# Softmax block kernel: sums of values in 64x32 tiles, one half of the keys at a time

## The chip, the cores and the metric

The kernel runs on one core of one Trainium2 chip. The metric is the device time of one execution in microseconds (us). The core's TensorE (PE) multiplies, and its weight loads are shown on their own row (PEld). VectorE (DVE), ScalarE (ACT), GpSimd (POOL) and the DMA queues, here issued by SyncE (SP), do the rest.

## The reference

One transformer block with an adaptive layer norm on 2048 rows of 512 values: 32 heads of 16 values, then a layer of 1792 hidden units.

```python
mod = (silu(c) @ w_mod).reshape(1, 6, 1, 512)          # sa, ca, ga, sb, cb, gb
h = layernorm(x) * (1 + ca) + sa
q, k, v = split(h @ wqkv)                              # 32 heads, 16 values each
p = softmax(q @ k.T * 16**-0.5)                        # 2048 x 2048 for each head
x = x + ga * ((p @ v) @ wo)
h = layernorm(x) * (1 + cb) + sb
x = x + gb * (gelu(h @ w1 + b1) @ w2 + b2)
```

All arrays are float32.

## The kernel before

The attention is cut into 32 units: four blocks of 512 queries (`TB`) times eight groups of four heads. Each unit runs through 16 chunks of 128 keys, so that the main loop has 32 x 16 = 512 steps. Before it, the inputs, the first projections and the first maxima are prepared; after it, the last block of rows goes through the output projection and the two layers of the feed-forward part.

A step works at three things in turn for attention.

- `exp_mm` (L589) makes scores with the keys on the partitions: 128 keys x 512 queries for one head. Its operands are 50 rows high (three parts of a split product of 16 rows each, and two rows that subtract the maximum). A head lies on partitions 0 to 63 or 64 to 127, so that a product uses one half of the rows of the array, in a 64x128 tile. ACT then takes the exponential into a tile `p` (L594), from a ring of twelve. Four such products belong to a step.
- `mx_mm` (L393) makes scores of a coming unit with the queries on the partitions, 48 rows high and again in a 64x128 tile. DVE reduces each to a maximum for its 128 queries (L398). Four belong to a step.
- `pv_step` (L618) multiplies the four tiles `p` of the step before with the values: 128 keys high, 32 columns wide for each head (16 values, a column of ones that gives the sum of the exponentials, and padding). The four heads stand in four 128x32 tiles side by side, all 128 rows high, and add into one bank of PSUM over the 16 chunks. These operands are full float32, and every product shows as two records in the profile.

After the sixteenth chunk `attn_out` copies the bank to SBUF by ACT (L606) and sends it to memory.

Beside that runs work of the other matrix products, "bg": the remaining projections, the output projection and the feed-forward part, as groups of split products that add to one bank each. They too are cut into halves of 64 rows (L287, `bg_mm`), because they are meant to stand in one half of the array while scores stand in the other. `half_step` issues six of them (`RUN`) in one step, all on one half, which changes with each step, and puts a score product on the other half behind each. When it has issued what the step owes, it calls `pv_step`.

The order in which the engines take all this is the order of the calls (`manual_schedule`). `later(n, f)` puts an action n exponentials later. `saw` notes the first ACT instruction behind a run of bg products; the run on the other half waits for it, since both halves add to one bank.

The eight banks of PSUM in the loop are dealt out by rings:

```python
ring("e", (0, 1, 2))
ring("mx", (3, 4, 5))
ring("pv", (6,))
ring("bg", (7,))
```

Of the kernel before, what the change touches and what calls it, by code (L numbers as in the profile page):

```python
# [7 lines left out]
F32 = mybir.dt.float32  # L8
FR = mybir.dt.float32r
AF = mybir.ActivationFunctionType  # L10
ALU = mybir.AluOpType
# [4 lines left out]
P = 128  # L16
# [8 lines left out]
TB = S // NB  # L25
HS = S // 2
NKC = S // P
NG = H // 4
NU = NB * NG
VW = DH + 1  # L30
# [10 lines left out]
RUN = 6  # L41
# [8 lines left out]
def block_kernel(ctx: ExitStack, tc: tile.TileContext, x, wqkv, wo, w1, b1, w2, b2, c, w_mod, out):  # L50
    nc = tc.nc
    te, ve, ac, gp, sy = nc.tensor, nc.vector, nc.scalar, nc.gpsimd, nc.sync
    ctx.enter_context(tc.manual_schedule())

    def pool(name, bufs=1, **kw):
        cm = tc.tile_pool(name=name, bufs=bufs, **kw)
        return cm, cm.__enter__()
# [8 lines left out]
    def bank(i, name):  # L66
        return bank_pools[i].tile([P, TB], F32, tag=f"bank{i}", name=name)
# [3 lines left out]
    def ring(name, ids):  # L71
        rings[name], turn[name] = list(ids), 0

    def take(name):
        ids = rings[name]
        turn[name] += 1
        return bank(ids[(turn[name] - 1) % len(ids)], name)
# [6 lines left out]
    ou_d = [dram.tile([NG, P, TB], F32, name=f"ou{b}") for b in range(NB)]  # L84
# [25 lines left out]
    kqcm, kqpool = pool("kq")  # L110
# [166 lines left out]
    def later(n, f):  # L277
        hooks.setdefault(clock["t"] + n, []).append(f)

    def advance():  # L280
        clock["t"] += 1
        for f in hooks.pop(clock["t"], []):
            f()
# [67 lines left out]
    def kh(u, h):  # L351
        return khalf[(2 * u + h) % 5]
# [28 lines left out]
    xc, red, mrows = [0, 0], {}, set()  # L381

    def mx_mm(a):

        u, i = XFIRST[xc[a]] if xc[a] < 64 else divmod(xc[a], 32)
        xc[a] += 1
        kr, p, qc = i // 8, (i // 4) % 2, i % 4
        if u not in mxp:
            mxp[u] = small.tile([P, 16, 4], F32, tag="mxp", name="mxp")
            red[u] = 0  # L390
        ps = take("mx")
        r0 = a * 64
        te.matmul(ps, qst[u][r0 : r0 + KR, p, qc * P : (qc + 1) * P],  # L393
                  kh(u, kr // 2)[r0 : r0 + KR, p, (kr % 2) * TB : (kr % 2 + 1) * TB], start=True, stop=True)
        hc = (a * 2 + p) * 4 + qc

        def reduce():
            ins = ve.tensor_reduce(mxp[u][:, hc, kr : kr + 1], ps, axis=AX.X, op=ALU.max, negate=True)  # L398
            red[u] += 1
            if red[u] == 64:  # L400
                max_rows(u)
            return ins

        return reduce

    def max_rows(u):
        m = mn[u % 2]
        ve.tensor_reduce(m[:, :16], mxp.pop(u), axis=AX.X, op=ALU.min)
        mt = small.tile([P, 32], F32, tag="mt", name="mt")
        ve.transpose(mt, m)  # L410
        m2 = small.tile([P, 2, 32], FR, tag="m2", name="m2")
        gp.tensor_copy(m2[:, 0], mt)  # L412
        gp.tensor_tensor(m2[:, 1], mt, m2[:, 0].bitcast(F32), op=ALU.subtract)

        def store():
            for i in range(2):
                sy.dma_start(m_d[u][i].rearrange("x b j -> b x j"), m2[:, i].bitcast(F32))

        def load():
            mrows.add(u)  # L420
            for a in range(2):
                r0 = a * 64 + KR
                sy.dma_start(qst[u][r0 : r0 + 2].bitcast(F32).rearrange("s p t -> s (p t)"),
                             m_d[u][:, a * 8 : a * 8 + 8].rearrange("s x b j -> s (x b j)"))

        if u:
            later(5, store)
        else:
            store()
        later(11 if u else 2, load)  # L430
# [104 lines left out]
    ppcm, ppool = pool("p", bufs=12)  # L535
    vg, pt = {}, {}
# [31 lines left out]
        preps.append((w2[f * P : (f + 1) * P, :], w2_d[f], gb_b))  # L568


    ring("e", (0, 1, 2))
    ring("mx", (3, 4, 5))
    ring("pv", (6,))
    ring("bg", (7,))
    ec, begun = [0, 0], [0]
    cur = {"pv": 0}

    def exp_mm(a, bk="e"):

        s, p = divmod(ec[a], 2)  # L580
        while begun[0] < min(ec) // 2 + 1:
            begun[0] += 1
            step_start(begun[0] - 1)
        ec[a] += 1
        u, kc = divmod(s, NKC)
        assert u in mrows, (u, ec, xc, red, clock["t"])
        r0 = a * 64
        ps = take(bk)
        te.matmul(ps, kh(u, kc // 8)[r0 : r0 + KX, p, (kc % 8) * P : (kc % 8 + 1) * P], qst[u][r0 : r0 + KX, p],  # L589
                  start=True, stop=True)  # L590

        def act():
            t = ppool.tile([P, TB], F32, tag="p", name="p")
            saw(ac.activation(t, ps, AF.Exp, scale=SCALE))  # L594
            pt[4 * s + p * 2 + a] = t
            advance()

        return act

    done = [-1] * NB  # L600
    ready = []

    def attn_out(u, pv):
        qb, g = divmod(u, NG)
        o = kqpool.tile([P, TB], F32, tag="osb", name="osb", bufs=1)
        saw(ac.activation(o, pv, AF.Copy))  # L606
        later(2, lambda: sy.dma_start(ou_d[qb][g], o))
        if g % 2:
            later(8, lambda: ready.append((qb, g // 2)))

    def pv_step():
        s = cur["pv"]
        cur["pv"] += 1
        u, kc = divmod(s, NKC)
        if kc == 0:
            cur["ps"] = take("pv")
        for j in range(4):
            te.matmul(cur["ps"][32 * j : 32 * (j + 1)], vg[u][:, kc, j * VW : j * VW + 32], pt.pop(4 * s + j),  # L618
                      start=kc == 0, stop=kc == NKC - 1)
        if kc == NKC - 1:  # L620
            vg.pop(u)
            attn_out(u, cur["ps"])


    pools = {}
# [68 lines left out]
    stream, at = [], 0  # L694
    for b in range(NB):
        stream += [(b, "o", k) for k in range(KC)]
        at = 0
        for lo, hi in PARTS:
            top = min(hi + AHEAD, NF)
            stream += [(b, 1, i) for i in range(at, top)] + [(b, 2, i) for i in range(lo, hi)]  # L700
            at = top
# [172 lines left out]
    act = {"g": None}  # L874

    def saw(ins):

        if act["g"] and not act["g"]["seen"]:
            act["g"]["seen"] = ins.ins

    def bg_mm(h):

        g = act["g"]
        terms, bk, evac = g["group"]
        i = g["at"][h]
        if i == len(terms):
            return False
        if g["n"] == 0:
            g["ps"] = take(bk)
        ins = mm(g["ps"], terms[i], g["n"], 2 * len(terms), slice(h * 64, h * 64 + 64)).ins  # L890
        if g["n"] and g["half"] != h:
            tc.add_manual_dep(ins, g["seen"].name, AFTER, reason="both halves of the rows add to one bank")
        g["half"], g["seen"] = h, None
        g["at"][h] += 1
        g["n"] += 1
        if g["n"] == 2 * len(terms):
            evac(g["ps"])
            act["g"] = None
        return act["g"] is not None

    def half_step(hs):
        h = hs % 2
        if h:
            wload()
        if act["g"] is None:
            j = next(jobs, None)
            if callable(j):
                j()
            elif j is not None:
                act["g"] = {"group": j, "at": [0, 0], "n": 0, "seen": None}  # L910
        nx = min(64 * NU, LEAD + 4 * (hs + 1))
        ne = 4 * (hs + 1)

        def x_ok(a):
            return sum(xc) < nx and xc[a] < 32 * NU

        def e_ok(a):
            return sum(ec) < ne and ec[a] < 2 * NU * NKC

        more = act["g"] is not None  # L920
        free = not more
        k = 0
        while more and k < RUN:
            a = 1 - h
            more = bg_mm(h)
            if e_ok(a) and sum(ec) < ne - 1 and (k % 2 == 1 or not x_ok(a)):
                exp_mm(a)()
            elif x_ok(a):
                mx_mm(a)()
            k += 1  # L930
        while sum(ec) < ne or sum(xc) < nx:
            a = 0 if ec[0] <= ec[1] else 1
            fs = []
            if sum(ec) < ne:
                fs.append(exp_mm(a, "bg" if free and sum(ec) == ne - 1 else "e"))
                if x_ok(1 - a):
                    fs.append(mx_mm(1 - a))
                elif e_ok(1 - a):
                    fs.append(exp_mm(1 - a))
            else:  # L940
                fs += [mx_mm(i) for i in range(2) if x_ok(i)]
            for f in fs:
                f()
        if hs:
            assert min(ec) >= 2 * cur["pv"] + 2
            pv_step()

    pend = []

# [12 lines left out]
        try_prep()  # L962

    for hs in range(NU * NKC):
        half_step(hs)
    if act["g"]:
        while bg_mm(1 - hs % 2):
            pass
    pv_step()
    while act["g"]:  # L970
        bg_mm(hs % 2)
    close(ppcm, vgcm)


    ring("bg", (0, 1, 2, 3, 4, 5, 7))
    tcm, tpool = pool("tail")
    extra += [tpool.tile([P, 2, D], FR, name=f"wt{i}") for i in range(6)]
    x2_t += [tpool.tile([P, D], F32, name=f"x2t{i}") for i in range(4)]
# [14 lines left out]
    left, j = True, None  # L993
    while left or j != "ffn":
        if j != "ffn":
            j = next(last)
# [3 lines left out]
        i = next(jobs, 0)  # L1000
# [32 lines left out]
```

## Time and profile before

| | |
|---|---|
| median of 3 runs | 1830.92 us (1827.09 to 1833.09) |
| profiled execution | 1831.95 us, span 1829.8 us |
| mean granted TensorE clock | 0.973 |
| PE busy | 1752.0 us, 96% |
| DVE busy | 1403.7 us, 77% |
| ACT busy | 1210.8 us, 66% |
| POOL busy | 602.5 us, 33% |

The profile is of one execution. The span runs from the first to the last instruction. In a timeline each row has a start and a length in us, the engine, the line of the kernel, the operation, what it writes and reads, the shape, and how many instructions are drawn together. Matmuls are pipelined: a record of 0.39 us does not keep its tile for that long, and the pace is read from the starts. The ends of matmuls are modelled.

### The profile page before, as it was taken

The page shows a single profiled execution, that of the slowest core. Times are in us where ns is not written, and L with a number is a line of the kernel's source. Part 1 is how long each engine was busy: PE and PEld are TensorE (multiplying, and loading weights), DVE is VectorE, ACT ScalarE, POOL GpSimd, SP SyncE. Part 2 cuts the span into 40 slices and gives each one's busy share as a digit, 9 for nine tenths or more (in the row PEclk, how much of TensorE's full clock was granted, in tenths as well). Part 3 has the DMA queues.
Part 4 walks back from the last instruction along what each step waited for, and adds up shares of the span by engine and source line. Part 5 has one row for each costly group of instructions (what it writes and reads, how often), then busy time and mean ns, then how long its engine had stood idle before and what let it go on. Part 6 is the DMA issues. An engine that isn't in the chain of part 4 may idle for free. (4 is left out here: it accounts for less than half of the span.)

```text
span 1829.8 us, 32358 instructions
## 1 busy us (share of the span) xinstructions
PE 1752.0 (96%) x12032; PEld 905.0 (49%) x12032; DVE 1403.7 (77%) x2347; ACT 1210.8 (66%) x2303; POOL 602.5 (33%) x640
## 2 busy tenths in 40 slices
PE   7798999999999899999999899999999899999899
PEld 5475444444434344444444344444444444445677
DVE  4466888888898788888899888888889888850232
ACT  2324777777676678778777688778776678777031
POOL 2413544543100246206410246306420136405420
PEclk9798999999899899999999899999999999999999
DMA  6647777777633434346446444336446434312544
GB/s 196 202 122 203 217 184 203 209 192 188 181 80 69 89 89 110 75 94 158 108 102 183 103 108 107 83 87 155 106 96 192 111 64 109 97 35 97 182 156 161
DMA packets 122906, 242.62 MB, mean 133 GB/s; under 512 B 30982, under 2 KB 50454, under 8 KB 122750
## 3 DMA queue, kind: packets, MB, share of 16 engines
q1 hardware_dynamic: 122750, 240.57, 50.3%
q8 instruction: 95, 1.56, 0.4%
q14 instruction: 61, 0.50, 0.1%
HBM read 187.61 MB, written 52.90 MB: 131 GB/s over the span
## 5 line engine op out<-in xcount | busy, mean ns | idle before, releaser
L398 DVE TENSOR_REDUCE mxp<-mx 128x1 f32<-128x512 f32 x2048 | 1272.7, 683 | 203.7 <-PE mx L393 184.0
L594 ACT ACTIVATE p<-e 128x512 f32<-128x512 f32 x1967 | 1029.4, 603 | 358.8 <-PE e L589 305.4
L393 PE MATMUL mx<-kh,qst 48*128 48x512 f32 x2048 | 873.8, 444 | 26.4 <-DVE mxp L398 19.9
L589 PE MATMUL e<-qst,kh 50*128 50x512 f32 x1967 | 716.9, 419 | 5.1 <-issue 4.8
L618 PE MATMUL pv<-p,vg 128*32 128x512 f32 x4096 | 553.9, 613 | 0.0
L589 PEld LDWEIGHTS e<-qst,kh 50*128 50x128 f32 x1967 | 359.7, 188 | 173.3 <-ACT p L594 150.8
L393 PEld LDWEIGHTS mx<-kh,qst 48*128 48x128 f32 x2048 | 376.7, 187 | 76.6 <-DVE mxp L398 71.0
L287 PE MATMUL bg<-w,g 64*128 64x512 f32 (+1 forms) x1020 | 274.3, 406 | 3.4 <-DVE x L830 1.0
L287 PE MATMUL bg<-pc,w 64*128 64x512 f32 (+1 forms) x984 | 270.3, 407 | 1.4 <-DVE x L830 0.7
L287 PEld LDWEIGHTS bg<-w,g 64*128 64x128 f32 (+1 forms) x1020 | 179.3, 186 | 146.3 <-ACT p L594 82.2
L287 PEld LDWEIGHTS bg<-pc,w 64*128 64x128 f32 (+1 forms) x984 | 169.5, 184 | 160.9 <-ACT p L594 98.8
L618 PEld LDWEIGHTS pv<-p,vg 128*32 128x32 f32 x4096 | 81.1, 108 | 129.6 <-issue 122.8
L412 POOL CAST m<-mt 128x32 fp32r<-128x32 f32 x32 | 6.7, 209 | 369.6 <-DVE mt L410 369.6
L287 PE MATMUL bg<-hThi,wqk 64*128 64x512 f32 x352 | 107.2, 424 | 0.3 <-ACT p L594 0.3
L804 POOL TENSOR_SCALAR s<-s 128x512 f32<-128x512 f32 x42 | 63.0, 1500 | 132.2 <-ACT s L802 124.0
L287 PEld LDWEIGHTS bg<-hThi,wqk 64*128 64x128 f32 x352 | 59.6, 188 | 80.5 <-ACT p L594 73.7
L797 POOL TENSOR_TENSOR s<-h 128x512 f32<-128x512 f32 x42 | 43.7, 1041 | 120.1 <-ACT h L796 119.9
L287 PE MATMUL bg<-wo,pc 64*128 64x512 f32 x288 | 81.9, 412 | 1.0
L287 PEld LDWEIGHTS bg<-wo,pc 64*128 64x128 f32 x288 | 49.5, 184 | 48.3 <-ACT p L594 27.7
L670 POOL TENSOR_TENSOR ob<-ob,rb 128x512 f32<-128x512 f32 x12 | 15.4, 1283 | 171.1 <-DMA rb<-rden 111.3
L773 ACT ACTIVATE h<-bg,modc 128x512 f32<-128x512 f32 x16 | 12.1, 778 | 67.5 <-PE bg L771 41.7
L807 POOL TENSOR_TENSOR g<-h,g 128x512 fp32r<-128x512 f32 x42 | 53.9, 1284 | 3.4
(128 smaller groups left out, 1267.3 us busy)
## 6 DMA issues: line engine op xcount, KB each, us to landing
kh<-qk SPq DMA_DIRECT2D x366, 128.0 KB
w<-w1s SPq DMA_DIRECT2D x56, 512.0 KB
w<-w2s SPq DMA_DIRECT2D x51, 512.0 KB
vg<-v SPq DMA_DIRECT2D x32, 664.0 KB
qk<-parts SPq DMA_DIRECT2D x32, 512.0 KB
qst<-qk SPq DMA_DIRECT2D x192, 64.0 KB
ou<-osb SPq DMA_DIRECT2D x32, 256.0 KB
wo<-wos SPq DMA_DIRECT2D x15, 512.0 KB
```

The lines of the kernel that those rows point to most:

```text
L287: return te.matmul(ps, term[0][r], term[1][r], start=i == 0, stop=i == n - 1)
L393: te.matmul(ps, qst[u][r0 : r0 + KR, p, qc * P : (qc + 1) * P], kh(u, kr // 2)[r0 : r0 + KR, p, (kr % 2) * TB : (kr % 2 + 1) * TB], start= ...
L398: ins = ve.tensor_reduce(mxp[u][:, hc, kr : kr + 1], ps, axis=AX.X, op=ALU.max, negate=True)
L412: gp.tensor_copy(m2[:, 0], mt)
L589: te.matmul(ps, kh(u, kc // 8)[r0 : r0 + KX, p, (kc % 8) * P : (kc % 8 + 1) * P], qst[u][r0 : r0 + KX, p], start=True, stop=True)
L594: saw(ac.activation(t, ps, AF.Exp, scale=SCALE))
L618: te.matmul(cur["ps"][32 * j : 32 * (j + 1)], vg[u][:, kc, j * VW : j * VW + 32], pt.pop(4 * s + j), start=kc == 0, stop=kc == NKC - 1)
L670: eng.tensor_tensor(ob, ob, rb, op=ALU.mult)
L773: ac.activation(h, ps, AF.Identity, scale=modc[:, 1, fc, 0:1], bias=modc[:, 1, fc, 1:2])
L797: gp.tensor_tensor(s, h, h, op=ALU.mult)
L804: gp.tensor_scalar(s, s, 1.0, None, op0=ALU.add)
L807: gp.tensor_tensor(g[:, 1], h, g[:, 0].bitcast(F32), op=ALU.subtract)
```

## The change

The sums of values are no longer taken over all 128 keys of a chunk at once. `pv_half(h)` takes the four heads over the 64 keys on partitions 0 to 63 or 64 to 127, in 64x32 tiles; the two halves add into two banks of their own, bank 6 and bank 2. Bank 2 is taken from the ring of scores for the exponentials, which is left with two. `attn_out` copies both banks by ACT and adds them on POOL, and what follows it is put off by four exponentials more.

`half_step` becomes `step`, with an order that is written out. With bg products, and h for their half and o for the other: bg beside a maximum, bg beside an exponential's score, both once more, then the sum of values on o, two bg and a score on h, the sum of values on h, and three scores on o. Without bg products: the sum on h, four scores on o, the sum on o, four scores on h. The sums lag two steps behind the scores instead of one. The half on which the six bg products stand still changes with each step.

```diff
-    ring("e", (0, 1, 2))
+    ring("e", (0, 1))
     ring("mx", (3, 4, 5))
-    ring("pv", (6,))
+    ring("pv", (6, 2))
     ring("bg", (7,))
...
     def attn_out(u, pv):
         qb, g = divmod(u, NG)
-        o = kqpool.tile([P, TB], F32, tag="osb", name="osb", bufs=1)
-        saw(ac.activation(o, pv, AF.Copy))
-        later(2, lambda: sy.dma_start(ou_d[qb][g], o))
+        o = [pl.tile([P, TB], F32, tag=f"osb{h}", name=f"osb{h}", bufs=1) for h, pl in enumerate((kqpool, ppool))]
+        for h in range(2):
+            saw(ac.activation(o[h], pv[h], AF.Copy))
+        gp.tensor_tensor(o[0], o[0], o[1], op=ALU.add)
+        later(6, lambda: sy.dma_start(ou_d[qb][g], o[0]))
...
-    def pv_step():
-        s = cur["pv"]
-        cur["pv"] += 1
+    def pv_half(h):
+        s = pvc[h]
+        pvc[h] += 1
         u, kc = divmod(s, NKC)
-        if kc == 0:
-            cur["ps"] = take("pv")
+        assert min(ec) >= 2 * s + 2
+        if u not in sums:
+            sums[u] = [take("pv"), take("pv")]
+        r = slice(h * 64, h * 64 + 64)
         for j in range(4):
-            te.matmul(cur["ps"][32 * j : 32 * (j + 1)], vg[u][:, kc, j * VW : j * VW + 32], pt.pop(4 * s + j),
+            te.matmul(sums[u][h][32 * j : 32 * (j + 1)], vg[u][r, kc, j * VW : j * VW + 32], pt[4 * s + j][r],
                       start=kc == 0, stop=kc == NKC - 1)
...
+        h = act["g"]["n"] // RUN % 2 if more else 0
...
+        def pv(a):
+            if hs > 1:
+                pv_half(a)
...
+        o = 1 - h
+        if more:
+            order = ((bg,), (x, o), (bg,), (e, o), (bg,), (x, o), (bg,), (e, o), (pv, o), (bg,), (bg,), (e, h),
+                     (pv, h), (x, o), (e, o), (x, o))
+        else:
+            order = ((pv, h), (x, o), (e, o), (x, o), (e, o), (pv, o), (x, h), (e, h), (x, h), (e, h))
+        for f, *a in order:
+            f(*a)
```

`x` issues a product for a maximum, `e` one for an exponential, `bg` one of the six products of other work.

More of the change, by code (lines that the diff above doesn't have):

```diff
@@ L568, in block_kernel @@
         preps.append((w2[f * P : (f + 1) * P, :], w2_d[f], gb_b))
-    ring("e", (0, 1, 2))
+    ring("e", (0, 1))
     ring("mx", (3, 4, 5))
-    ring("pv", (6,))
+    ring("pv", (6, 2))
     ring("bg", (7,))
     ec, begun = [0, 0], [0]
-    cur = {"pv": 0}
+    pvc, sums = [0, 0], {}
     def exp_mm(a, bk="e"):
@@ L604, in attn_out @@
         qb, g = divmod(u, NG)
-        o = kqpool.tile([P, TB], F32, tag="osb", name="osb", bufs=1)
-        saw(ac.activation(o, pv, AF.Copy))
-        later(2, lambda: sy.dma_start(ou_d[qb][g], o))
+        o = [pl.tile([P, TB], F32, tag=f"osb{h}", name=f"osb{h}", bufs=1) for h, pl in enumerate((kqpool, ppool))]
[3 more added lines that the diff above has]
+        later(6, lambda: sy.dma_start(ou_d[qb][g], o[0]))
         if g % 2:
-            later(8, lambda: ready.append((qb, g // 2)))
-    def pv_step():
-        s = cur["pv"]
-        cur["pv"] += 1
+            later(12, lambda: ready.append((qb, g // 2)))
+    def pv_half(h):
+        s = pvc[h]
+        pvc[h] += 1
         u, kc = divmod(s, NKC)
-        if kc == 0:
-            cur["ps"] = take("pv")
+        assert min(ec) >= 2 * s + 2
+        if u not in sums:
+            sums[u] = [take("pv"), take("pv")]
+        r = slice(h * 64, h * 64 + 64)
         for j in range(4):
-            te.matmul(cur["ps"][32 * j : 32 * (j + 1)], vg[u][:, kc, j * VW : j * VW + 32], pt.pop(4 * s + j),
+            te.matmul(sums[u][h][32 * j : 32 * (j + 1)], vg[u][r, kc, j * VW : j * VW + 32], pt[4 * s + j][r],
                       start=kc == 0, stop=kc == NKC - 1)
-        if kc == NKC - 1:
-            vg.pop(u)
-            attn_out(u, cur["ps"])
+        if min(pvc) > s:
+            for j in range(4):
+                pt.pop(4 * s + j)
+            if kc == NKC - 1:
+                vg.pop(u)
+                attn_out(u, sums.pop(u))
     pools = {}
@@ L899, in bg_mm, with step @@
         return act["g"] is not None
-    def half_step(hs):
-        h = hs % 2
-        if h:
+    def step(hs):
+        if hs % 2:
             wload()
@@ L910, in half_step, with x, e, bg @@
                 act["g"] = {"group": j, "at": [0, 0], "n": 0, "seen": None}
+        more = act["g"] is not None
+        h = act["g"]["n"] // RUN % 2 if more else 0
         nx = min(64 * NU, LEAD + 4 * (hs + 1))
         ne = 4 * (hs + 1)
[L914 to L928, printed above, removed]
+        def x(a):
+            if sum(xc) < nx and xc[a] < 32 * NU:
                 mx_mm(a)()
[L930 to L933, printed above, removed]
+        def e(a):
             if sum(ec) < ne:
[L935 to L946, printed above, removed]
+                a = a if ec[a] < 2 * NU * NKC else 1 - a
+                exp_mm(a, "bg" if not more and sum(ec) == ne - 1 else "e")()
+        def pv(a):
+            if hs > 1:
+                pv_half(a)
+        def bg():
+            bg_mm(h)
+        o = 1 - h
[6 more added lines that the diff above has]
+            f(*a)
+        while sum(xc) < nx:
+            x(0 if xc[0] <= xc[1] else 1)
+        assert sum(ec) == ne
     pend = []
@@ L964, in block_kernel @@
     for hs in range(NU * NKC):
[L965 to L969, printed above, removed]
+        step(hs)
+    for h in range(2):
+        pv_half(h)
+    h = act["g"]["n"] // RUN % 2 if act["g"] else 0
+    while act["g"] and act["g"]["at"][h] < len(act["g"]["group"][0]):
+        bg_mm(h)
+    for i in range(2):
+        pv_half(i)
     while act["g"]:
-        bg_mm(hs % 2)
+        bg_mm(1 - h)
     close(ppcm, vgcm)
-    ring("bg", (0, 1, 2, 3, 4, 5, 7))
+    ring("bg", (0, 1, 3, 4, 5, 7, 2))
     tcm, tpool = pool("tail")
```

## The prediction

> **What bounds the kernel now.** I read the page's first part, then its groups, then who waited for whom on TensorE, then a steady stretch of the timeline.
>
> ```profile
> span 1829.8 us, 32358 instructions
> PE 1752.0 (96%) x12032; PEld 905.0 (49%) x12032; DVE 1403.7 (77%) x2347; ACT 1210.8 (66%) x2303; POOL 602.5 (33%) x640
> ...
> L398 DVE TENSOR_REDUCE mxp<-mx 128x1 f32<-128x512 f32 x2048 | 1272.7, 683 | 203.7 <-PE mx L393 184.0
> L594 ACT ACTIVATE p<-e 128x512 f32<-128x512 f32 x1967 | 1029.4, 603 | 358.8 <-PE e L589 305.4
> ```
> ```profile
> PE mx L393 <- DVE mxp L398: 19.9, 13, 4.6
> ```
>
> TensorE is busy for 96% of the span, its longest wait in total is 19.9 us, and DVE idles for 203.7 us in front of the maxima, mostly for TensorE. The bound is TensorE's stream. A busy share does not say how well it is packed, so I read two steps by starts.
>
> ```profile
> 901.91 1.07 PE L618 MATMUL pv<-p,vg 128*32 128x512 f32 x8
> 902.90 0.50 PE L287 MATMUL bg<-w,g 64*128 64x512 f32 x1
> 902.91 0.49 PE L393 MATMUL mx<-kh,qst 48*128 48x512 f32 x1
> 903.24 0.40 PE L589 MATMUL e<-qst,kh 50*128 50x512 f32 x1
> 903.24 0.62 PE L287 MATMUL bg<-w,g 64*128 64x512 f32 x2
> 903.48 0.40 PE L393 MATMUL mx<-kh,qst 48*128 48x512 f32 x1
> 903.71 0.39 PE L287 MATMUL bg<-w,g 64*128 64x512 f32 x1
> ...
> 904.17 0.39 PE L287 MATMUL bg<-w,g 64*128 64x512 f32 x1
> 904.18 0.69 PE L589 MATMUL e<-qst,kh 50*128 50x512 f32 x2
> 904.41 0.48 PE L393 MATMUL mx<-kh,qst 48*128 48x512 f32 x1
> 904.82 1.06 PE L618 MATMUL pv<-p,vg 128*32 128x512 f32 x8
> 905.82 0.50 PE L287 MATMUL bg<-w,g 64*128 64x512 f32 x1
> ```
> ```profile
> 902.90 0.18 PEld L287 LDWEIGHTS bg<-w,g 64*128 64x128 f32 x1 [0.84 <-ACT p L594]
> 902.90 0.18 PEld L393 LDWEIGHTS mx<-kh,qst 48*128 48x128 f32 x1
> 903.01 0.19 PEld L287 LDWEIGHTS bg<-w,g 64*128 64x128 f32 x1
> ```
> ```profile
> L618 PE MATMUL pv<-p,vg x4096: 592/616/1062, 162.8 to 1688.8; 128*32 128x512 f32 x196
> ```
>
> From one block of sums to the next is 904.82 - 901.91 = 2.91 us: the step. Seven pairs of 64x128 products stand in it, each pair one product on either half of the rows. Inside, pairs start every (904.41 - 903.24) / 5 = 0.234 us, so 7 x 0.234 = 1.64 us. The block of sums costs the rest, **1.27 us**. Its eight records (two for each of four products; 4096 in 512 steps) come in two waves: the block lasts 1.07 us and a record 0.592 to 0.617 us, so the second four start about 0.46 us after the first, and two waves are 0.92 us. The remaining 0.35 us lies at the borders. The last pair before the sums is followed only after 0.41 us instead of 0.23; the first pair behind them comes 0.99 us after their start, and the second pair 0.34 us after that instead of 0.23. The weight row tells why: the weight rows idle for 0.84 us during the sums, and the first weights of the next shape load at 902.90, when the sums are through. Between pairs of one shape weights load ahead (903.01 for 903.24). So at a change of the tile's shape TensorE runs empty before even weights of the new shape move.
>
> How many steps are of this kind:
>
> ```profile
> L287 PE MATMUL bg<-pc,w 64*128 64x512 f32 x960 | 264.5, 408 | 1.4 <-DVE x L830 0.7 <-ACT p L594 0.6
> L287 PE MATMUL bg<-w,g 64*128 64x512 f32 x816 | 226.0, 409 | 3.4 <-DVE x L830 1.0
> L287 PE MATMUL bg<-hThi,wqk 64*128 64x512 f32 x352 | 107.2, 424 | 0.3 <-ACT p L594 0.3
> L287 PE MATMUL bg<-wo,pc 64*128 64x512 f32 x288 | 81.9, 412 | 1.0
> ...
> L287 PE MATMUL bg<-hTlo,wqk 64*128 64x512 f32 x176 | 47.7, 390 | 0.0
> ```
>
> The half products of other work number 960 + 816 + 352 + 288 + 176 = 2592, six to a step: **432 steps with them, 80 without**. A step without them:
>
> ```profile
> 1449.24 2.48 DVE L398 TENSOR_REDUCE mxp<-mx 128x1 f32<-128x512 f32 x4 [0.18 <-PE mx L393]
> ...
> 1450.42 1.07 PE L618 MATMUL pv<-p,vg 128*32 128x512 f32 x8
> ...
> 1453.15 1.06 PE L618 MATMUL pv<-p,vg 128*32 128x512 f32 x8
> ```
>
> It takes 1453.15 - 1450.42 = 2.73 us, near the 2.48 us of its four maxima on DVE. 432 x 2.91 + 80 x 2.73 = 1475 us, against 1526 us from the first sums to the last (162.8 to 1688.8). The other 51 us are stalls between.
>
> **The change part by part.**
>
> *The sums cut in halves.* Four products 128 rows high become eight, 64 high, and each still streams 512 columns in two waves. So there are two blocks of 0.92 us, each filling half the array, where one block filled all of it. That costs nothing if the other half works meanwhile, and 0.92 us a step if it does not. The order written out offers that: three 64x128 products stand behind each block on the other half. All hangs on whether a 64x32 product on one half and a 64x128 product on the other are in the array together.
>
> The trace of before has no 64x32 product. The nearest rows are the borders above: between 128x32 and 64x128 even the weights wait until the array is empty. There both shapes share rows, here they don't. But a conflict of rows alone would not hold back weights, which between equal shapes on the same rows load ahead; it looks like a barrier on the shape. The Trainium skill, TensorEngine Tiling (Array Packing), section Tiling Modes, Key Properties, says that changing the tiling mode, not just the tile, drains the engine, and it lists 64x128 and 64x32 as two configurations; the trace agrees for 128x32 against 64x128 (0.35 us of borders a step), and by this rule the sum is the 2770 us below, without it the 1700 us of the first rival.
>
> I take the barrier. Then a step has four borders instead of two, and nothing stands beside the sums. A step with other work becomes: three scores on o together with the next step's first four bg and four scores. The next step's bg stands on the old o, so the longer chain there is 3 + 4 = 7 products, 7 x 0.234. Then a block; then two bg and a score, all on one half, 3 x 0.234; then a block. That is 10 x 0.234 + 2 x 1.27 = 4.88 us, **1.97 us more**, of which 0.70 is the three products that lost their partners and 1.27 the second block. 432 x 1.97 = 851 us. A step without other work: 8 x 0.234 + 2 x 1.27 = 4.41 us, 1.68 more, 80 times: 134 us.
>
> The block's price has two ends: 1.27 us, as above; and 0.99 us, from its start to the next product's, if nothing else of the borders is added. The low end gives 4.32 and 3.85 us, so 432 x 1.41 + 80 x 1.12 = 699 us instead of 985. I take 1.27, since it is the row's full price with the same neighbours, 64x128 on both sides.
>
> *The stalls.* In steps of 4.9 us DVE (2.48 us) and ACT are far from late, and loads have longer to land, so I take the 51 us off; the other end is to leave them.
>
> *Two banks for scores instead of three, twelve tiles p with a lag of two steps.* A bank is held for a product (0.39 us) and an exponential (0.60): 0.99 / 2 = 0.50 us a score, four in 1.98 us. Steps of 2.91 or 4.88 us hide that; at 2.5 us it would show whenever ACT does something else. The twelve tiles now hold exactly the three steps between a score and the end of its sums, so the first exponential of a step waits for the block on h of the step before; ACT's copies for other work queue behind it. In the order of issue that block stands ahead of the exponential's own product anyway, so with a barrier the wait is over when the product ends. Zero here.
>
> *The copy of the sums.*
>
> ```profile
> L606 ACT ACTIVATE osb<-pv 128x512 f32<-128x512 f32 x32 | 19.3, 603 | 5.0 <-PE pv L618 3.1
> L670 POOL TENSOR_TENSOR ob<-ob,rb 128x512 f32<-128x512 f32 x12 | 15.4, 1283 | 171.1 <-DMA rb<-rden 111.3
> ```
>
> 32 more copies of 0.60 us on ACT and 32 additions of about 1.28 us on POOL. ACT is busy 66% and POOL 33%, so both hide, but POOL is in order: the addition waits for both copies, and the products and subtractions of the hidden layer queue behind it. They have actions of ten exponentials (over 7 us) between them, which cover it. The store of the sums waits four exponentials more on SP's queue. Only the last unit has no cover: 0.6 + 1.28, about 2 us at the start of the tail. The rest of the tail uses other shapes and is as before.
>
> The sum: 1831.95 (the profiled execution, 1 us above the median of 1830.92) + 851 + 134 + 2 - 51 = **2768, say 2770 us**. Its own range: 1832 + 699 + 2 - 51 = 2480 with the low block, and 1832 + 987 = 2819 with all stalls kept, to which I add 30 for what the steps may lose elsewhere: 2480 to 2850.
>
> **The rivals.**
>
> *No barrier between 64x32 and 64x128; faster.* Both halves run through 7 products and one block with no borders: 7 x 0.234 + 0.92 = 2.56 us, just over DVE's 2.48. 432 x 0.35 = 151 us less: 1683. At that pace DVE, the two banks and TensorE take turns in being late by up to some 0.15 us a step (half the slack gone), 65 us, so 1683 to 1748, and I put it at 1700. For it: 48- and 50-row products already stand beside 64-row ones in one pace, so the halves are independent in one shape. Against: the weights held back at every border seen. It decides from the point where a block's borders cost under 0.35 us in each half while the other half goes on.
>
> *Together in the array, but no gain; slower by a little.* Each half pays its own borders (0.35 us a step, as now), so the step stays at 2.91, and the two banks show behind each ACT copy of another product: at most 0.60 us for each of 432 / 4 groups, 65 us, so 1834 to 1899. If moreover products start in the order of issue, whatever half they are on, then the three behind a block wait until its second wave has started, and a step is 10 x 0.234 + 0.92 = 3.26 us: 151 us more, 1985. I put this at 1900. The Trainium skill, TensorE: Matmul & The Clock Gate, Part 3, The mechanism, holds that matmuls start and end strictly in program order, which would make the 1985 the likelier end here; no row here shows one half waiting in that way.
>
> **How the numbers follow.** The barrier 0.50, together without gain 0.19, no barrier 0.31. One case of each sign has much of the chance, and nothing lies between but the second rival. The range leaves out what may lie above 2850 and the lower half of the faster case: 1695 to 2850; the likeliest case's own range is 2480 to 2850. A run can tell 0.3%, 5.5 us, from no change. Faster 0.31 is the first rival. A small part of the second ends within 0.3%: 0.03. Slower: 0.66.
>
> **What would show it.** Right: in the timeline of the changed kernel no 64x128 product starts while a block of sums streams; blocks are 0.9 to 1.3 us long, two to a step, with weight loads idle over each; steps of about 4.9 us; DVE falls to about half busy; the first two bg behind a block stand alone. For the first rival: 64x32 records and 64x128 records start within one another, steps of 2.5 to 2.7 us, DVE over 90% busy. For the second: they overlap, but the step stays near 2.9 or 3.3 us, with waits of scores on ACT. I am wrong altogether if the block on 64 rows is not as long as that on 128, or if products of other work fall behind and run in the tail.

## The result, and the profile after

The changed kernel takes 4634.92 us (median of 4 runs, 4630.36 to 4638.2) against 1831.35 us before: 2.534 times as long (95% interval 2.528 to 2.540). Forecast were 2770 us, 1695 to 2850. The direction was right, the size was not.

From the profile's page of the changed kernel, the parts that answer to those of before; the two digit rows are PE's busy share and the granted clock in 40 slices:

```profile
span 4632.8 us, 40374 instructions
...
PE 4566.7 (99%) x16128; PEld 1879.4 (41%) x16128; DVE 1509.0 (33%) x2347; ACT 1390.9 (30%) x2335; POOL 640.9 (14%) x672
...
PE   7999999999999999999999999999999999999999
...
PEclk8655555555555555555555555555555555555559
...
L398 DVE TENSOR_REDUCE mxp<-mx 128x1 f32<-128x512 f32 x2048 | 1370.3, 689 | 2687.1 <-PE mx L393 2666.6
...
L623 PE MATMUL pv<-p,vg 64*32 64x512 f32 x8192 | 1972.3, 1057 | 0.0
```

TensorE is busy for 99%, DVE for a third, and DVE waits 2687 us in front of the maxima, for TensorE. The new thing is the clock row. Before, it stood at 9 in nearly all of the loop, with a few slices at 8:

```profile
PEclk9798999999899899999999899999999999999999
```

Now it stands at 5 from the start of the loop to its end. By stages (from, to, length, busy us of each engine with counts, granted clock, DMA):

```profile
170.00:500.00 330.00, 329.31 (x1147) 130.35 (x1144) 102.45 (x156) 98.95 (x168) 56.86 (x60) 0.50 0.28 71
...
2000.00:3000.00 1000.00, 995.74 (x3451) 394.80 (x3450) 331.79 (x511) 303.63 (x512) 140.17 (x140) 0.50 0.19 42
...
4490.00:4632.00 142.00, 127.33 (x526) 101.12 (x526) 39.09 (x59) 27.68 (x41) 40.16 (x36) 0.94 0.50 169
```

One step in TensorE's timeline:

```profile
2300.94 1.93 PE L623 MATMUL pv<-p,vg 64*32 64x512 f32 x8
2302.80 0.80 PE L393 MATMUL mx<-kh,qst 48*128 48x512 f32 x2
2303.39 0.80 PE L589 MATMUL e<-qst,kh 50*128 50x512 f32 x2
2303.82 0.62 PE L393 MATMUL mx<-kh,qst 48*128 48x512 f32 x1
2304.24 0.62 PE L287 MATMUL bg<-w,g 64*128 64x512 f32 x1
...
2305.10 1.05 PE L287 MATMUL bg<-w,g 64*128 64x512 f32 x2
2306.08 1.93 PE L623 MATMUL pv<-p,vg 64*32 64x512 f32 x8
2307.94 1.22 PE L287 MATMUL bg<-w,g 64*128 64x512 f32 x2
2308.96 0.62 PE L589 MATMUL e<-qst,kh 50*128 50x512 f32 x1
2309.51 1.93 PE L623 MATMUL pv<-p,vg 64*32 64x512 f32 x8
```

Weight loads at the first border:

```profile
2300.94 0.20 PEld L623 LDWEIGHTS pv<-p,vg 64*32 64x32 f32 x8 [0.65 <-issue]
2302.80 0.30 PEld L393 LDWEIGHTS mx<-kh,qst 48*128 48x128 f32 x2 [1.66 <-issue]
```

Two blocks of sums stand in a step, nothing starts while one streams, and no weights load for 1.66 us. That is the barrier as forecast. But the step, 2309.51 - 2300.94, is 8.57 us and not 4.88. Products on one half follow one another every 0.42 to 0.43 us (2303.82, 2304.24) instead of 0.234, and a block takes 1.86 us to the next product instead of 0.99.

The first rows also show something of the order. The two `mx` at 2302.80 are on different halves. In the order of issue the one on the old h stands behind a score, a maximum and a bg on the old o, and it starts before all three.

### The profile page after: what moved, and what is told of

Same layout as the page of the kernel before. It is cut to its first block, busy times and chain, and to the rows that moved or that the text cites. A ratio compares the mean times of both kernels' runs of the same rounds, so it can differ in the third digit from the quotient of the medians.

```text
span 4632.8 us, 40374 instructions
## 1 busy us (share of the span) xinstructions
PE 4566.7 (99%) x16128; PEld 1879.4 (41%) x16128; DVE 1509.0 (33%) x2347; ACT 1390.9 (30%) x2335; POOL 640.9 (14%) x672
## 4 chain that ended last, share of the span: by engine, by line
PE 95%; issue 2%; DMA 1%; POOL 1%; DVE 1%; ACT 0%; SPq 0%; ACTq 0%; POOLq 0%; DVEq 0%
PE pv L623 40%; PE bg L287 23%; PE mx L393 15%; PE e L589 14%; PE pr L287 1%; PE bg L589 1%; PE bg L779 0%; DVE mxp L398 0%; ACT p L594 0%; DMA wraw<-in_A_wqkv_dram 0%; DMA rden<-dn 0%; DMA xin<-in_A_x_dram 0%; POOL hTlo L269 0%; DMA wt<-w2s 0%; DMA ou<-osb 0%
## 5 line engine op out<-in xcount | busy, mean ns | idle before, releaser
L594 ACT ACTIVATE p<-e 128x512 f32<-128x512 f32 x1965 | 1172.5, 597 | 2795.4 <-PE e L589 2420.2
L623 PE MATMUL pv<-p,vg 64*32 64x512 f32 x8192 | 1972.3, 1057 | 0.0
L393 PE MATMUL mx<-kh,qst 48*128 48x512 f32 x2048 | 1144.0, 727 | 5.3 <-DVE mxp L398 5.3
L589 PE MATMUL e<-qst,kh 50*128 50x512 f32 x1965 | 1043.5, 663 | 7.2 <-issue 7.2
L393 PEld LDWEIGHTS mx<-kh,qst 48*128 48x128 f32 x2048 | 489.4, 291 | 1017.9 <-issue 911.5
L589 PEld LDWEIGHTS e<-qst,kh 50*128 50x128 f32 x1965 | 602.2, 309 | 97.6 <-issue 40.9
L287 PE MATMUL bg<-pc,w 64*128 64x512 f32 (+1 forms) x984 | 506.1, 648 | 3.0 <-ACT p L594 2.3
L287 PE MATMUL bg<-w,g 64*128 64x512 f32 (+1 forms) x1008 | 469.5, 603 | 0.0
L623 PEld LDWEIGHTS pv<-p,vg 64*32 64x32 f32 x8192 | 201.2, 136 | 660.5 <-issue 638.0
L287 PEld LDWEIGHTS bg<-pc,w 64*128 64x128 f32 (+1 forms) x984 | 293.9, 318 | 322.1 <-issue 267.9
```

Of the source, the lines that this page charges most:

```text
L287: return te.matmul(ps, term[0][r], term[1][r], start=i == 0, stop=i == n - 1)
L623: te.matmul(sums[u][h][32 * j : 32 * (j + 1)], vg[u][r, kc, j * VW : j * VW + 32], pt[4 * s + j][r], start=kc == 0, stop=kc == NKC - 1)
```

## The experiments

Two things were to be told apart: what keeps the two halves from working together, and what holds the clock down. The shares in use below are estimates, worked out with the prediction's durations at full clock: 1.64 us of pairs, 0.92 us for a block. They hold for steps with other work. A row of the array counts as in use while any of its columns works; a cell is one row by one column.

### Both halves of the sums at once

```diff
-  order = (... (pv, o), (bg,), (bg,), (e, h), (pv, h), (x, o), (e, o), (x, o))
+  order = (... (bg,), (x, o), (bg,), (e, o), (e, h), (x, o), (pv, o), (pv, h))   # and alike without bg
```

> The sums stay cut into two 64x32 halves with two banks, but both halves are issued one behind the other at the end of the step, and the order of the rest is as before the change. Shape barrier (64x32 and 64x128 never together, equal shapes on the two halves together): the two blocks lie on one another, 0.9 to 1.0 us for both, two borders a step, step 2.9 us, clock back near 0.97, 1835 us (1825 to 1860). Rival, the halves of the sums cannot stand beside anything because products are held in the order of issue: the two blocks follow one another, 1.9 us at full clock, step 3.8 us, 2250 us or more, and perhaps still half the clock.

2060.45 us, ratio 1.127 (1.124 to 1.130), clock 0.977. TensorE's timeline:

```profile
1004.13 1.09 PE L623 MATMUL pv<-p,vg 64*32 64x512 f32 x16
1005.15 0.50 PE L287 MATMUL bg<-w,g 64*128 64x512 f32 x1
...
1006.41 0.39 PE L287 MATMUL bg<-w,g 64*128 64x512 f32 x1
1006.63 0.98 PE L589 MATMUL e<-qst,kh 50*128 50x512 f32 x2
1007.12 0.50 PE L393 MATMUL mx<-kh,qst 48*128 48x512 f32 x1
```

Sixteen records take 1.09 us, where eight took 1.07 before: both halves run together when their shape is the same. The clock is back. The time is neither theory's. The pair of scores at 1006.63 lasts 0.98 us, its second product half a microsecond late. That points to the two score banks, which a later run takes alone (Two banks for scores alone).

### The sums of two steps in one block

The kernel before, with `pv_step` called twice in every second step:

```diff
-        if hs:
+        if hs and hs % 2 == 0:
             pv_step()
+            pv_step()
```

> The kernel before the change, 128x32 tiles, but the sums of two steps are issued one behind the other in every second step, so that the loop has 256 blocks instead of 512 and half the borders. Border theory (0.35 us a block): 216 x 0.35 = 76 us less in the steps with other work, nothing in the others, which DVE bounds: 1755 us (1745 to 1790). Rival, DVE runs dry during a block of 1.9 us since three banks of maxima are ready at most, and gives it back: 1820 to 1840 us.

1984.04 us, ratio 1.085 (1.080 to 1.091): the rival's side, and worse than the rival's 1820 to 1840 us. TensorE's block, and DVE's row around it:

```profile
1204.07 1.92 PE L618 MATMUL pv<-p,vg 128*32 128x512 f32 x16
```
```profile
1202.71 2.48 DVE L398 TENSOR_REDUCE mxp<-mx 128x1 f32<-128x512 f32 x4
1206.49 0.69 DVE L398 TENSOR_REDUCE mxp<-mx 128x1 f32<-128x512 f32 x1 [1.30 <-PE mx L393]
```

DVE has nothing for 1.30 us, for the three banks are empty before the block ends. Then it needs 2.5 us a step again. In all, DVE waits 312.0 us for a maximum's product here, against 184.0 before, and the granted clock is 0.952 against 0.973. Halving the number of borders gains nothing in this kernel; how much a border alone is worth can't be read here.

### The same order in one shape

```diff
-        for j in range(4):
-            te.matmul(sums[u][h][32 * j : 32 * (j + 1)], vg[u][r, kc, j * VW : j * VW + 32], pt[4 * s + j][r], ...)
+        v0 = min(kc, NKC - 2) * VG
+        te.matmul(sums[u][h], vg[u].rearrange("p k e -> p (k e)")[r, v0 : v0 + P], pt[4 * s][r], ...)
...
+            ve.tensor_scalar(dn, dn, 1.0, None, op0=ALU.max)     # before the reciprocal
```

> The changed kernel with its order and banks, but each block of sums is one product in a 64x128 tile (64 keys of one head by 128 columns of values) instead of four in 64x32 tiles; it takes the same two waves of 512 columns. The values of the sums mean nothing then, and three heads are left out. No shape changes in the step. Shape theory: the blocks run beside scores on the other half, clock near 0.97, and the step falls to what the two score banks allow, 2.6 to 3.4 us: 1700 to 2060 us. Rival, the blocks keep out the other half in any shape, because a float32 product of two waves holds up what is issued behind it: still four gaps a step, 2500 us or more.

1911.29 us, ratio 1.046 (1.042 to 1.050), clock 0.973.

```profile
902.49 0.59 PE L623 MATMUL pv<-p,vg 64*128 64x512 f32 x1
902.50 0.39 PE L287 MATMUL bg<-pc,w 64*128 64x512 f32 x1
902.85 0.50 PE L589 MATMUL e<-qst,kh 50*128 50x512 f32 x1
902.92 0.59 PE L623 MATMUL pv<-p,vg 64*128 64x512 f32 x1
902.95 0.79 PE L393 MATMUL mx<-kh,qst 48*128 48x512 f32 x1
```

With the same order, banks, halves and number type, a bg starts at 902.50 beside the block's first wave, and a maximum at 902.95 beside the second. What keeps the halves apart in the changed kernel is the shape of the tile, not the rows, the order or float32. One thing changes with the shape in this run: a block is one product instead of four side by side. Whether four would stand apart for their number alone was not run.

### Two banks for scores alone

```diff
-    ring("e", (0, 1, 2))
+    ring("e", (0, 1))
```

> The kernel before the change with one edit, the ring of banks for scores of exponentials cut from three to two, as the change does. If the 1.127 of both_halves comes from the banks: 2000 to 2080 us, TensorE waiting for ACT. If it comes from something else in the cut sums (lag, copies, second bank): 1830 to 1870 us.

2040.92 us, ratio 1.116 (1.113 to 1.119). Waits of the weight row for scores, before and then in this run:

```profile
PEld e L589 <- ACT p L594: 150.8, 465, 0.8
```
```profile
PEld e L589 <- ACT p L594: 369.1, 970, 1.3
```

The bank that the change takes from the scores costs 209 us by itself in a kernel at this pace, and explains nearly all of `both_halves`. If the two costs simply add, the cut sums with their copies and lag are about 1%.

### Fill the blocks

The changed kernel, with each block running both halves, so that TensorE does more:

```diff
-        r = slice(h * 64, h * 64 + 64)
-        for j in range(4):
+        for i in range(2):
+            r = slice(i * 64, i * 64 + 64)
+            for j in range(4):
```

> Order and borders of the changed kernel, but each of the two blocks of a step runs both halves of the sums, so that every sum is made twice (numerators and denominators both double, the quotient stays). Four borders a step as in the changed kernel; of the array's time at full clock (1.64 + 2 x 0.92) / 4.88 = 71% is filled instead of (1.64 + 0.92) / 4.88 = 52%. Theory A, the clock follows how much of the array is in use: clock near 0.97, step about 4.9 us, 2770 us. Theory B, the clock is held down by the borders, at which the array runs empty: clock 0.53, step 8.6 us, 4635 us.

2838.21 us, clock 0.967.

```profile
1199.80 1.09 PE L625 MATMUL pv<-p,vg 64*32 64x512 f32 x16
1200.82 0.73 PE L287 MATMUL bg<-w,g 64*128 64x512 f32 x2
...
1201.72 1.09 PE L625 MATMUL pv<-p,vg 64*32 64x512 f32 x16
1202.74 0.51 PE L393 MATMUL mx<-kh,qst 48*128 48x512 f32 x2
...
1204.69 1.09 PE L625 MATMUL pv<-p,vg 64*32 64x512 f32 x16
```

The step is 4.89 us: the forecast one, with all four borders. The whole is 68 us above theory A's 2770 us. More work makes the kernel 1797 us shorter. Theory B, that borders hold the clock down, has fallen.

### A quarter of the array

The kernel before with `pv_step` as

```diff
+            for i in range(3):
+                for j in range(2):
+                    te.matmul(cur["ps"][32 * j : 32 * (j + 1)], vg[u][:64, kc, j * VW : j * VW + 32],
+                              pt[4 * s + j][:64], start=False, ...)
```

for all chunks but the first, and with a small operation before the reciprocal that keeps it from dividing by zero.

> The kernel before with its one block of sums a step, two borders, but in 15 of 16 steps the block holds only two heads over the first 64 keys, a quarter of the array, issued three times (the rest of the sums is left out). At full clock a step takes 1.64 + 3 x 0.92 + 0.35 = 4.75 us and fills (1.64 + 3 x 0.92 / 4) / 4.75 = 49% of the array's time, with two borders. Theory A, the clock follows the use of the array: clock near 0.53, step about 8.3 us, 4300 us (4000 to 4600). Theory B, borders hold the clock down, fewer of them here in the same time than in the changed kernel: clock near 0.97, 2675 us.

2712.63 us, clock 0.938. Theory A had asked for 0.53. Theory B's 2675 us is near, but `blocks_filled` contradicts that theory. Two stretches (columns as in the stages above):

```profile
176.00:865.00 689.00, 681.39 (x3652) 263.38 (x3650) 399.45 (x665) 339.50 (x655) 150.72 (x166) 0.99 0.42 108
866.00:1036.00 170.00, 170.00 (x552) 62.05 (x550) 58.18 (x89) 54.99 (x99) 31.71 (x32) 0.53 0.19 43
```

The same steps run for 689 us at 0.99 and then for 170 us at 0.53: a step with other work takes 8.54 us in the second stretch (blocks at 902.85 and 911.39) and 4.55 us soon after it (1040.34 and 1044.89). The clock fell in steps without other work, at about 855 us, and stayed low through steps with it. The one full block in 16 steps does not explain the high clock: of four rises in the loop, two come at or just behind such a block and two do not. By the number of cells in use (49%) it should have been lower than the changed kernel; so either something other than cells is counted, or the clock is a state with a memory. Four more runs went after that.

### Fill a few steps

`blocks_filled` with `for i in range(2) if both else (h,)`, where `both` is `4 <= kc < 8`, and in a second kernel `kc == 4 and u % 8 == 0`.

> The changed kernel, but in chunks 4 to 7 of each unit both blocks run both halves of the sums (these keys count twice, which changes the output). Theory H, the clock is a state: it is let up by a dense stretch, and then held by a use of 52% until something empties the array for long: clock 0.9 or more also in the other 12 steps of a unit, about 2800 to 3100 us. Theory L, the clock follows the use of the last few microseconds: up in the 4 filled steps, down again within 20 us, 4 x 4.9 + 12 x 8.57 us a unit: 3900 to 4200 us, mean clock 0.6 to 0.65.

> As filled_4_of_16, but only one step in the whole of units 0, 8, 16 and 24 is filled (chunk 4), four of 512 steps. Theory H: the clock rises there and stays up for hundreds of us, mean clock 0.75 or more, under 3400 us. Theory L: 4600 to 4640 us, clock 0.53.

The first: 3431.45 us, clock 0.766, between the two theories.

```profile
705.00:802.00 97.00, 97.00 (x716) 43.59 (x714) 50.66 (x85) 49.80 (x88) 26.50 (x30) 1.00 0.47 117
810.00:1265.00 455.00, 454.22 (x1640) 164.06 (x1632) 164.15 (x247) 142.08 (x240) 24.68 (x28) 0.50 0.21 45
1530.00:1976.00 446.00, 446.00 (x3111) 199.28 (x3109) 239.32 (x396) 227.39 (x400) 99.45 (x101) 1.00 0.32 69
```

The trace's clock rises eleven times in the loop, each time in a chunk 4 to 6, so on filled steps or just behind, and falls in chunks 8 to 14, 0 and 3. From 1530 to 1976 us it holds through six units, three quarters of whose steps are not filled. The second: 4551.73 us, clock 0.539; it rose in two of its four filled steps and held for 27 and 75 us. So in these runs the changed kernel's use of the array does hold the clock up for a while, but does not lift it. Theory H is right in kind and wrong in size; theory L alone is not enough either.

### A denser order

```diff
-  order = (... four pairs ..., (pv, o), (bg,), (bg,), (e, h), (pv, h), (x, o), (e, o), (x, o))
+  order = (... six pairs ..., (pv, o), (e, h), (pv, h), (x, o))
```

> The changed kernel with four borders a step as before, but all six bg stand beside a score each, in one stretch of six pairs in front of the block on o; one score is left between the blocks and one behind. At full clock a step is 8 x 0.234 + 2 x 1.27 = 4.41 us and fills (1.64 + 0.92) / 4.41 = 58% of the array's time (changed: 52%, quarter_blocks: 49%). Theory D, the clock comes up again on a dense stretch of some microseconds, which six pairs (2.6 us at half clock) and the score behind the last block give as the seven pairs of quarter_blocks do: clock 0.9 or more, 2550 to 2750 us. Theory M, the mean use has to be well above that of the changed kernel, as in blocks_filled (71%): the clock stays at 0.53, about 4100 us.

3973.55 us, clock 0.585:

```profile
180.00:3840.00 3660.00, 3645.11 (x14786) 1395.01 (x14783) 1352.33 (x2110) 1301.61 (x2215) 559.50 (x574) 0.56 0.22 52
```

```profile
PEclk8755579755555555555555555555699555555569
```

The clock is low for most of the loop, as theory M said, but not for all of it: the clock row shows two stretches at full clock, about 190 and 245 us long, without any denser step to start them. Six pairs in a row do not keep it up, so theory D does not hold for six. That a longer dense stretch would do it is not ruled out. Here 58% of the cells are in use and the clock is low; in `quarter_blocks` 49%, and it is high. Mean use of cells is not what counts. A share of rows, whatever their columns, would put the kernels that repeat one step in order, and that could be tried. It would not place `filled_4_of_16`: its mean share is (4 x 71% + 12 x 52%) / 16 = 57%, less than here, and its clock, 0.766, is higher.

### One head in the filled blocks

`blocks_filled` with `for j in range(1 if kc else 4)`, and the small operation before the reciprocal.

> blocks_filled again, with both halves of the rows in each of the two blocks of a step, but in 15 of 16 chunks with one head of four, so with a quarter of the columns (the rest of the sums is left out). Time and borders stay as in blocks_filled. Share of the array's cells in use at full clock: (1.64 + 2 x 0.92 / 4) / 4.88 = 43%, less than in the changed kernel (52%). Share of its rows in use, whatever the columns: (1.64 + 2 x 0.92) / 4.88 = 71%, as in blocks_filled. By rows the runs so far stand in order: changed 52% (clock 0.53), six_pairs 58% (0.59), quarter_blocks (1.64 + 1.38) / 4.75 = 64% (0.94), blocks_filled 71% (0.97); by cells they don't (quarter_blocks 49%). Theory R, the clock follows the rows in use: 0.94 or more, 2800 to 2900 us. Theory C, it follows the cells: 0.53, about 4600 us.

2770.1 us, clock 0.978, a little under theory R's 2800 us:

```profile
180.00:2650.00 2470.00, 2442.08 (x11459) 1057.78 (x11456) 1292.31 (x2128) 1273.80 (x2217) 574.29 (x585) 0.99 0.33 78
```

| kernel | rows in use | cells in use | mean clock | us |
|---|---|---|---|---|
| changed | 52% | 52% | 0.527 | 4635 |
| six_pairs | 58% | 58% | 0.585 | 3974 |
| quarter_blocks | 64% | 49% | 0.938 | 2713 |
| blocks_filled | 71% | 71% | 0.967 | 2838 |
| one_head_filled | 71% | 43% | 0.978 | 2770 |
| before | 88% | 88% | 0.973 | 1832 |

With fewer cells in use than in the changed kernel the clock is full, because both halves of the rows are at work in the blocks. Theory C has fallen. Rows in use put these six kernels in order but for the last percent. What is shown is that idle rows in the blocks hold the clock down. By which measure is open: the longest stretch with both halves at work orders the six alike (four pairs in the changed kernel, six, seven, and then the kernels whose blocks use all rows too), and in `filled_4_of_16` the rises come on the dense steps.

No kernel beat the one before. The runs point to one shape for everything, but a sum of values in a 64x128 tile holds one head where four now stand side by side, so it would take four times the stream; no run shows what that costs.

## Why the prediction was wrong

**The barrier** was right, and its price too. Nothing starts beside a 64x32 block, and `one_shape` shows that the same order does run beside in one shape. The forecast step was 4.88 us; `blocks_filled`, with the same borders at full clock, shows 4.89. The forecast time was 2768 us; `one_head_filled`, with the same order, borders and block lengths, took 2770.1. That it comes within 2 us is luck in part, since `blocks_filled`, with the same step, took 2838.21. The Trainium skill, TensorEngine Tiling (Array Packing), section Tiling Modes, Key Properties, had it that a change of mode, not just of tile, drains the engine; the trace agrees also for tiles on different rows (1.66 us without a weight load).

**The step that failed** is one not written down: that the durations of before, read at a granted clock of 0.973, hold in the new order. They did not: the clock was 0.50 through the loop, and the step took 8.57 us instead of 4.88. Where the prediction multiplied 10 x 0.234 + 2 x 1.27 it should have asked what the clock does when for most of the step one half of the rows stands idle. Of the 2803 us added, some 940 us (2770 - 1832) are the barrier, and some 1865 us (4635 - 2770) the clock. This split is an estimate from `one_head_filled`; with `blocks_filled` it is some 1006 and 1797 us. The only room that the range left for it was the "30 for what the steps may lose elsewhere".

The Trainium skill, TensorE: Matmul & The Clock Gate, Part 1, says that a monitor of activity sets the clock to half or full, and that a busy window of about 3.4 us brings it up. The trace agrees in the two values (0.50 and 1.00 in the stages). It disagrees if busy means that products follow one another: TensorE was busy for 99% of 4.6 ms here, and the clock stayed down. The measurement decides: idle rows count.

**The two score banks** were put at zero for steps of 2.91 us, from 0.99 / 2 = 0.50 us a score. That took scores as evenly spread; but in the kernel before the four scores of a step start within 1.16 us (903.24 to 904.40), and the banks cost 209 us there. In the changed kernel, with 8.57 us a step, the zero held: the weight row waits 5.7 us in all for an exponential to free a score's bank. The first rival's 1700 us would have met that too: `one_shape`, which has no barrier, took 1911.

**The order.** The second rival's end of 1985 us took products as starting in the order of issue. The `mx` that started at 2302.80 ahead of three products on the other half shows that they do not, within one shape.

**The copies** were rightly small: 64 on ACT at 0.60 us and 32 additions on POOL at 1.28 us. They are off the path but for the last addition, at 4490.52 us, which the prediction had counted in its 2 us.

## What to carry to other kernels

Before cutting a product into smaller tiles to set it beside others, check that all of them have one shape: here a different number of columns was enough to keep idle rows out. And when an order leaves half of the rows idle for microseconds, don't carry over durations read at full clock; ask whether the clock will hold. Where a step must run half empty, repeated work in the idle rows may be cheaper than the idleness, as 2838 us against 4635 show here. Price a bank taken from a ring by the cluster in which its products come, not by their mean rate.

## What was not expected of the hardware

- In kernels that repeat one step the clock followed the rows in use, not the cells and not the busy share: 0.978 at 43% of the cells, 0.527 at 52%, with 71% and 52% of the rows.
- At 52, 58 and 64% of the rows both clocks occur for the same steps, for tens to hundreds of microseconds (the unfilled steps of `filled_4_of_16`, `six_pairs`, and 689 us at 0.99, 170 us at 0.53 in `quarter_blocks`). At what use, over what time, it rises and falls is open.
- In one shape a float32 product in two waves runs beside products of the other kind, its waves 0.43 us apart (902.49 and 902.92 in `one_shape`): the number type made no border.
